# An attention and feed-forward kernel on one core: statistics in single items, later blocks normalised on ScalarE, the last output-weight chunk fetched sooner, the last projections moved to even tiles

## The chip, the core and the metric

The kernel runs on one core of a Trainium2 chip. The metric is device time in microseconds (us). Times are the median of several executions; one further execution was profiled, and everything called a row, a view or the trace comes from that one. TensorE does the matrix products (PE in the profile, its weight loads PEld), VectorE is DVE, ScalarE is ACT, GpSimd is POOL, and SyncE (SP) issues all DMAs, one after the other in program order.

## The reference, cut to what matters

A pre-norm transformer layer on 2048 tokens of width 576, all in float32: attention with 32 heads of width 18 that share one key and one value head, then a bilinear feed-forward network (FFN) with 4608 hidden features.

```python
h  = x + attention(layernorm(x)) @ wo          # 32 heads x 18 = 576 columns
n  = layernorm(h)                              # mean, variance, (h - mean) / sqrt(var + 1e-5)
h2 = h + ((n @ w_gate) * (n @ w_up)) @ w_down  # 576 -> 4608 -> 576
```

## The kernel before

**Precision and blocks.** Each float32 operand of a product is split in a rounded part and a remainder (`split`, L86: a cast on ScalarE or GpSimd, then a subtraction on VectorE), and a product is the sum of three. The 2048 tokens are cut in four blocks of 512, numbered 0 to 3. In a block, four heads make a group, so there are eight groups; a "pair" (`pair`, L456) is one key tile for two heads: two score products and one exponential on ScalarE over 128x1024 (L477).

**The FFN loop.** `ffn(b)` (L794) runs 36 tiles f = 0 to 35 of 128 hidden features. A tile has 27 steps j, each a gate and an up product (L814) on the two halves of the array; then ScalarE copies the gate sum out of PSUM (L840, the "g copy", one per tile) and VectorE multiplies it with the up sum (L844, "hf"). Two tiles make one pair for the product with w_down. After an odd tile VectorE prepares that pair (`left`, L705: four sums of halves, then a split); after the next even tile `down` (L720) runs 42 products in 14 groups, each added to the residual by VectorE (L777) or by ScalarE and GpSimd (L781, L782). So even tiles end with `down`, and odd tiles end with `left`.

**Attention of later blocks between.** While `ffn(b)` runs, the pairs of block b+1 (and, at the end, the first ones of b+2) are issued between its steps, up to eight or nine a tile (`on`, L801). They run out in `ffn(2)` near tile 24; from there on a tile has only its own work, its two sums lie in another PSUM tile ("gu"), and `down` comes ahead of the g copy instead of behind hf.

**The list of small work.** What a finished head group needs is put on a list, `self.aux`, with the round from which it is due and, for some, a condition. `run_aux` (L499) is called at step 12 of each tile ("within") and at the end of each tile but the last of a block; a call counts one round and runs at most one due item. Items with a condition run at tile ends alone. The items, for block b:

- `normalise(b, g)` (L509): divides a group's output by its sums, transposes it on VectorE and lets SP send it to its rows of `ob`; for groups 1, 3, 5 and 7 it also fetches the next chunk of wo (`load_wo`, L564) and puts `chunk` on the list.
- `chunk(b, c)` (L543): splits chunk c of 128 rows, on ScalarE and VectorE. Chunk 4, the last 64 rows, also fetches its own part of wo (L548).
- `split_wo` (L569), at the end of each `run_aux`: splits a fetched chunk of wo on GpSimd and VectorE, from two rounds after its fetch, into the only buffer for it.
- `project(b, c)` (L593): multiplies chunk c with wo into eight PSUM tiles of 128x288 (24 products, 16 for chunk 4; L608); VectorE adds each to the residual h of block b (L609). Three PSUM buffers take turns, so the fourth tile waits for the first addition.
- `all_statistics(b)` (L629), after the last chunk: per token tile two `bn_stats` and one `bn_aggr` (L103, L104), four token tiles, then 1/sqrt(var) in 13 tiny instructions (`rstd`, L106).

**From block to block.** In tile 35, at step 6, `normal(b+1)` (L634) makes the normalised tokens: four VectorE instructions of 128x576 (L640), each followed by a copy of its last 64 columns on GpSimd (L641). After tile 35, `spread(b+1)` (L644) transposes them on TensorE (L657; the tile with those copied columns comes first), and `down` of the last pair (L732) runs among these transposes. In block 0 the w_down weights are prepared once for all blocks, by GpSimd and VectorE in steps between the products of a pair's two tiles (`right_sums` and `right`, L894 and L907), and SP writes them back to DRAM.

**What sets the order.** The program is written out in this order by hand; each engine runs its own instructions in program order and waits at semaphores.

Of the kernel before, what the change touches and what calls it, by code (L numbers as in the profile page):

```python
# [58 lines left out]
class Block:  # L59
# [439 lines left out]
    def run_aux(self, limit=1, within=False):  # L499


        self.round += 1
        due = [x for x in self.aux if x[0] < self.round and (x[2] is None or not within and x[2]())][:limit]
        for x in due:
            self.aux.remove(x)
            x[1]()
        self.split_wo()

    def normalise(self, b, g, os_):  # L509
        if g == 0:  # L510
            self.ob = self.op.tile([P, 5, TB], F32, tag="ob", name=f"ob{b}")
        c = ({1: 0, 3: 1, 5: 2, 6: 3, 7: 4} if b == 0 else {1: 0, 3: 1, 5: 2, 7: 3}).get(g)
        if b and c is not None:
            self.load_wo(c)
        self.normal_heads(b, g, os_)
        del self.os[g]
        if c is not None:
            self.aux.append((self.round + (LANDING if b == 0 and c < 4 else 0), lambda: self.chunk(b, c), None))

# [23 lines left out]
    def chunk(self, b, c):  # L543

        if b == c == 0:
            self.oT = self.otp.tile([P, 8, TB], F32R, tag="oT", name=f"oT{b}")
        self.chunk_of(b, c)
        if b and c == 4:  # L548
            self.load_wo(c)
        self.aux.append((self.round, lambda: self.project(b, c),  # L550
                         lambda: b in self.h and (c in self.wos if b else self.n_pair >= self.wo_from)))

# [16 lines left out]
    def split_wo(self):  # L569

        if self.wo_r and not self.wos and self.wo_round + 1 < self.round:
            c = min(self.wo_r)
            w = self.wos[c] = self.wp.tile([P, 2, D], F32R, tag="wos", bufs=1, name=f"wos{self.round}_{c}")
            self.split(w[:, 0], w[:, 1], self.wo_r.pop(c), self.nc.gpsimd.tensor_copy)

    def load_wo_0(self):
# [16 lines left out]
    def project(self, b, c):  # L593
# [23 lines left out]
        if c == 4:  # L617
            if b == 0:
                self.normed[b] = self.mv, self.rstd(self.mv[:, :, 1], f"b{b}")
            else:  # L620
                self.aux.append((self.round, lambda: self.all_statistics(b), None))

# [5 lines left out]

    def all_statistics(self, b):  # L629
        for s in range(NQ):  # L630
            self.statistics(b, s)
        self.normed[b] = self.mv, self.rstd(self.mv[:, :, 1], f"b{b}")

    def normal(self, b):  # L634
# [3 lines left out]
        for s in range(NQ):  # L638
            xh = self.p_tile([P, 640], f"xh2_{b}_{s}") if b else self.wp.tile([P, 640], F32, tag="wdo", bufs=WD_BUFS, name=f"xh2_0_{s}")
            self.dve.tensor_scalar(xh[:, 0:D], h[:, s, :], mv[:, s, 0:1], rs[:, s:s + 1], ALU.subtract, ALU.mult)  # L640
            self.nc.gpsimd.tensor_copy(xh[:, D:], xh[:, 512:D])  # L641
            self.xh.append(xh)
# [151 lines left out]
    def ffn(self, b):  # L794
        pe, act, dve = self.pe, self.act, self.dve
        X, hid, todo = self.X, [], None
        for f in range(NF):
# [11 lines left out]
            for c in range(9):  # L809
                for wk, xk in ((0, 0), (0, 1), (1, 0)):  # L810
# [8 lines left out]
                    if j == 5 and k:  # L819
                        self.left_first(n_ - 1, hid[0])  # L820
                    if j == 12:
                        self.run_aux(within=True)
                    if b == 0 and self.first:
# [7 lines left out]
                    if j == 21 and b == f == 0:  # L831
                        self.flush(len(self.pend))
                    if j == 6 and last:
                        self.normal(b + 1)
                    j += 1
# [94 lines left out]
    def begin(self, first):  # L930
# [5 lines left out]
        self.n_pair, self.half, self.pend, self.aux, self.round = 0, [], [], [], 0  # L936
        self.p_next, self.wo_from, self.due = -1, 10 ** 6, 0.0

# [219 lines left out]
```

## Time and profile before

| | us |
|---|---|
| median of 3 executions (2342.1 to 2344.63) | 2344.12 |
| the profiled execution | 2342.39 |
| its span, from the first to the last instruction | 2340.6 |
| ScalarE busy in it | 1433.3 |
| VectorE busy in it | 1210.6 |
| GpSimd busy in it | 684.0 |

The difference of 1.8 us between the profiled execution's time and its span lies outside the first and the last instruction. In a row of a group, "xN | a, b | c" is the number of instructions, their busy us, the mean ns of one, and the us for which the engine stood idle just before them. In a row of the timeline the first two numbers are start and duration in us, and "[a <-X]" is the idle time before it and what ended it.

### The profile page before, as it was taken

The page shows a single profiled execution, that of the slowest core. Times are in us where ns is not written, and L with a number is a line of the kernel's source. Part 1 is how long each engine was busy: PE and PEld are TensorE (multiplying, and loading weights), DVE is VectorE, ACT ScalarE, POOL GpSimd, SP SyncE. Part 2 cuts the span into 40 slices and gives each one's busy share as a digit, 9 for nine tenths or more (in the row PEclk, how much of TensorE's full clock was granted, in tenths as well). Part 3 has the DMA queues.
Part 4 walks back from the last instruction along what each step waited for, and adds up shares of the span by engine and source line. Part 5 has one row for each costly group of instructions (what it writes and reads, how often), then busy time and mean ns, then how long its engine had stood idle before and what let it go on. Part 6 is the DMA issues. An engine that isn't in the chain of part 4 may idle for free.

```text
span 2340.6 us, 46187 instructions
## 1 busy us (share of the span) xinstructions
PE 2283.8 (98%) x18225; PEld 1602.6 (68%) x18225; DVE 1210.6 (52%) x2175; ACT 1433.3 (61%) x1868; POOL 684.0 (29%) x873
## 2 busy tenths in 40 slices
PE   5999999999999999999999999999999989999998
PEld 4344445666677667667777777776777678888887
DVE  7333345565656566444444445444444466556655
ACT  4888886667676765567676766667776623223332
POOL 3100001444455453222222222212222233333332
PEclk9999999999999999999999999999999999999999
DMA  4222222344444442633433443533333345655553
GB/s 140 72 65 81 75 90 81 128 147 143 148 143 143 141 146 93 197 119 123 128 123 117 123 135 107 180 109 121 113 126 122 109 145 188 203 183 171 168 180 116
DMA packets 127225, 306.59 MB, mean 131 GB/s; under 512 B 15679, under 2 KB 16447, under 8 KB 126999
## 3 DMA queue, kind: packets, MB, share of 16 engines
q1 hardware_dynamic: 126999, 303.54, 40.1%
q8 instruction: 146, 2.39, 0.4%
q14 instruction: 80, 0.66, 0.1%
HBM read 234.00 MB, written 55.67 MB: 124 GB/s over the span
## 4 chain that ended last, share of the span: by engine, by line


## 5 line engine op out<-in xcount | busy, mean ns | idle before, releaser
L477 ACT ACTIVATE P<-s 128x1024 f32<-128x1024 f32 x1024 | 1026.7, 1027 | 302.5 <-PE s L476 221.9
L814 PE MATMUL pg<-X,ws 64*128 64x512 f32 x2592 | 707.1, 391 | 0.0
L814 PE MATMUL pu<-X,ws 64*128 64x512 f32 x2592 | 707.0, 391 | 0.0
L814 PEld LDWEIGHTS pg<-X,ws 64*128 64x128 f32 x2592 | 481.4, 186 | 58.9 <-issue 1.2
L814 PEld LDWEIGHTS pu<-X,ws 64*128 64x128 f32 x2592 | 478.5, 186 | 36.7 <-DMA X<-X 0.4
L481 PE MATMUL acc<-P,V 128*32 128x512 f32 x4096 | 488.7, 598 | 0.9 <-ACT P L477 0.6
L476 PE MATMUL s<-q,kT 56*128 56x512 f32 x2048 | 436.8, 422 | 2.5 <-ACT P L477 1.8
L774 PEld LDWEIGHTS y<-wdo,room 128*128 128x128 f32 x2856 | 386.2, 188 | 48.4 <-issue 44.2
L774 PE MATMUL y<-wdo,room 128*128 128x288 f32 x2856 | 403.5, 300 | 1.1 <-DVE h L777 1.1
L781 ACT COPY tmp<-y 128x288 f32<-128x288 f32 x408 | 162.7, 400 | 342.0 <-PE y L774 326.9
L476 PEld LDWEIGHTS s<-q,kT 56*128 56x128 f32 x2048 | 194.0, 184 | 198.7 <-ACT P L477 114.4
L814 PE MATMUL gu<-X,ws 64*128 64x512 f32 x2592 | 303.1, 390 | 0.0
L782 POOL TENSOR_TENSOR x<-x,tmp 128x288 f32<-128x288 f32 x204 | 159.2, 810 | 445.5 <-ACT tmp L781 444.7
L481 PEld LDWEIGHTS acc<-P,V 128*32 128x32 f32 x4096 | 114.8, 109 | 249.2 <-issue 241.2
L814 PEld LDWEIGHTS gu<-X,ws 64*128 64x128 f32 x2592 | 248.9, 185 | 48.0 <-issue 5.2
L88 POOL CAST ws<-wr 128x1152 fp32r<-128x1152 f32 x144 | 171.6, 1191 | 329.7 <-PE pg L814 111.4
L782 POOL TENSOR_TENSOR h<-h,tmp 128x288 f32<-128x288 f32 x204 | 159.4, 812 | 371.0 <-ACT tmp L781 370.7
L89 DVE TENSOR_TENSOR ws<-wr,ws 128x1152 fp32r<-128x1152 f32 x144 | 204.4, 1419 | 82.4 <-POOL ws L88 82.4
L844 DVE TENSOR_TENSOR hf<-pu,g 128x512 f32<-128x512 f32 x96 | 66.3, 690 | 264.5 <-ACT g L840 261.2
L777 DVE TENSOR_TENSOR x<-x,y 128x288 f32<-128x288 f32 x272 | 117.4, 453 | 146.4 <-PE y L774 146.4
L777 DVE TENSOR_TENSOR h<-h,y 128x288 f32<-128x288 f32 x272 | 118.2, 454 | 114.9 <-PE y L774 112.2
L89 DVE TENSOR_TENSOR room<-S,room 128x1024 fp32r<-128x1024 f32 x68 | 86.0, 1265 | 149.2 <-ACT room L88 149.2
(169 smaller groups left out, 1734.6 us busy)
## 6 DMA issues: line engine op xcount, KB each, us to landing
wdo<-wd_dram SPq DMA_DIRECT2D x369, 288.0 KB
wr<-in_wgu_dram SPq DMA_DIRECT2D x144, 576.0 KB
wd_dram<-wdo SPq DMA_DIRECT2D x123, 288.0 KB
q<-q_dram SPq DMA_DIRECT2D x64, 216.0 KB
raw<-in_wd_dram SPq DMA_DIRECT2D x36, 288.0 KB
q_dram<-qs SPq DMA_DIRECT2D x16, 504.0 KB
X<-X SPq DMA_DIRECT2D x28, 256.0 KB
x<-in_x_dram SPq DMA_DIRECT2D x16, 288.0 KB
```

The source lines that it names most:

```text
L88: (copy or self.cast)(hi, src)
L89: self.dve.tensor_tensor(lo, src, f32(hi), ALU.subtract)
L476: self.pe.matmul(s_[:, i], self.kT[o:o + 56, t * P:(t + 1) * P], q[o:o + 56, pr], start=True, stop=True)
L477: self.act.activation(p_, s_, AF.Exp, scale=SCALE)
L481: self.pe.matmul(acc[32 * j:32 * j + 32, :], self.V[:, t, :], Ps[j // 2][:, j % 2, :], start=(t == 0), stop=(t == NT - 1), skip_group_chec ...
L774: pe.matmul(y[:, :HD], m[:, t * P:(t + 1) * P], k, start=(first and j == 0), stop=(j == 2), skip_group_check=True)
L777: dve.tensor_tensor(hs, hs, y[:, :HD], ALU.add)
L781: act.copy(z, y[:, :HD])
L782: pool.tensor_tensor(hs, hs, z, ALU.add)
L814: pe.matmul(ps, w[o:o + 64, wk, c], X[o:o + 64, xk, c], start=(j == 0), stop=(j == 26))
L844: dve.tensor_tensor(hf, pu, g, ALU.mult)
```

## The change

It has five parts, all in how the FFN blocks are served.

1. **Statistics in single items.** `all_statistics` becomes four items, one a token tile. For blocks 1 and 2 they can run within a tile or at its end. For block 3 they run only within odd tiles, two in one call, and the 13 instructions of `rstd` are an item of their own (`scales`). `scales` also makes -mean/sqrt(var), one more tiny instruction.
2. **Normalising on ScalarE.** For blocks 1 to 3, `normal` uses four ScalarE activations (Identity, with scale 1/sqrt(var) and bias -mean/sqrt(var)) in place of the four VectorE instructions. Block 0 stays on VectorE.
3. **wo sooner.** The fetch of wo's chunk 4 is issued right after the split of chunk 3, not by chunk 4's own item.
4. **Even ends.** The projections of block 3 run only at the ends of even tiles (`self.odd` holds whether the last finished tile was odd). Chunk 0 of later blocks is due two rounds later than before.
5. **Tile 35.** No item runs within the last tile of blocks 0 to 2. In block 0 all steps of `right` for the last pair are issued at step 6, ahead of `normal(1)`, and no longer between later steps.

In the order of the program this moves the items so ("end 8" is the end of tile 8, "in 8" its step 12; all other items stay where they were):

| item | before | after |
|---|---|---|
| block 1, in ffn(0): chunk 0, project 0 | end 6, end 7 | end 7, end 8 |
| wo chunk 4 fetched, project 4 | in 32, end 33 | in 31, end 32 |
| statistics of block 1 | all at end 34 | in 33, end 33, in 34, end 34 |
| block 2, group 0 normalised | in 34 of ffn(0) | in 0 of ffn(1) |
| block 2, in ffn(1): chunk 0, project 0 | end 3, end 4 | end 4, end 5 |
| wo chunk 4 fetched, project 4 | in 29, end 30 | in 28, end 29 |
| statistics of block 2 | all at end 31 | in 30, end 30, in 31, end 31 |
| block 3, group 0 normalised | in 31 of ffn(1) | in 32 of ffn(1) |
| block 3, group 1 normalised | in 35 of ffn(1) | in 0 of ffn(2) |
| block 3, in ffn(2): chunk 0 | in 0 | end 1 |
| projects 0 to 4 | ends 1, 9, 17, 25, 27 | ends 2, 10, 18, 26, 28 |
| wo chunk 4 fetched | in 26 | in 25 |
| statistics of block 3 | all in 28 | two in 29, two in 31, `scales` in 33 |

```diff
@@ run_aux
-        due = [x for x in self.aux if x[0] < self.round and (x[2] is None or not within and x[2]())][:limit]
+        due = [x for x in self.aux if x[0] < self.round and (x[2] is None or within == (x[2] == self.within) and x[2]())][:limit]
...
+    def within(self):
+        return not self.odd
@@ normalise
-            self.aux.append((self.round + (LANDING if b == 0 and c < 4 else 0), lambda: self.chunk(b, c), None))
+            self.aux.append((self.round + (LANDING if b == 0 and c < 4 else 2 if b and c == 0 else 0), lambda: self.chunk(b, c), None))
@@ chunk
-        if b and c == 4:
-            self.load_wo(c)
         self.aux.append((self.round, lambda: self.project(b, c),
-                         lambda: b in self.h and (c in self.wos if b else self.n_pair >= self.wo_from)))
+                         lambda: b in self.h and (c in self.wos and not (self.odd and b == NB - 1) if b else self.n_pair >= self.wo_from)))
@@ split_wo
             self.split(w[:, 0], w[:, 1], self.wo_r.pop(c), self.nc.gpsimd.tensor_copy)
+            if c == 3:
+                self.load_wo(4)
@@ project
-                self.aux.append((self.round, lambda: self.all_statistics(b), None))
+                last = b == NB - 1
+                for i in range(4):
+                    self.aux.append((self.round + i // 2, lambda i=i: self.some_statistics(b, i), self.within if last else None))
+                if last:
+                    self.aux.append((self.round + 2, lambda: self.scales(b), self.within))
...
+    def some_statistics(self, b, s):
+        self.statistics(b, s)
+        if s == NQ - 1 and b < NB - 1:
+            self.scales(b)
+
+    def scales(self, b):
+        mv, r = self.mv, self.rstd(self.mv[:, :, 1], f"b{b}")
+        self.dve.scalar_tensor_tensor(mv[:, :, 0], mv[:, :, 0], -1.0, r, ALU.mult, ALU.mult)
+        self.normed[b] = mv, r
@@ normal
-            self.dve.tensor_scalar(xh[:, 0:D], h[:, s, :], mv[:, s, 0:1], rs[:, s:s + 1], ALU.subtract, ALU.mult)
+            if b:
+                self.act.activation(xh[:, 0:D], h[:, s, :], AF.Identity, bias=mv[:, s, 0:1], scale=rs[:, s:s + 1])
+            else:
+                self.dve.tensor_scalar(xh[:, 0:D], h[:, s, :], mv[:, s, 0:1], rs[:, s:s + 1], ALU.subtract, ALU.mult)
@@ ffn
-                    if j == 12:
-                        self.run_aux(within=True)
+                    if j == 12 and not last:
+                        self.run_aux(2 if b == NB - 2 and k else 1, within=True)
...
                     if j == 6 and last:
+                        if b == 0 and self.first:
+                            drain(parts)
                         self.normal(b + 1)
...
+            self.odd = k
             if f < NF - 1:
                 self.run_aux()
```

More of the change, by code (lines that the diff above doesn't have):

```diff
@@ L627, in statistics @@
         self.ln_stats(self.h[b][:, s, :], self.mv[:, s, :], s, f"b{b}")
[L629 to L632, printed above, removed]
+    def some_statistics(self, b, s):
[6 more added lines that the diff above has]
+        self.normed[b] = mv, r
     def normal(self, b):
@@ L936, in begin @@
         self.n_pair, self.half, self.pend, self.aux, self.round = 0, [], [], [], 0
-        self.p_next, self.wo_from, self.due = -1, 10 ** 6, 0.0
+        self.p_next, self.wo_from, self.due, self.odd = -1, 10 ** 6, 0.0, 0
     def blocks(self):
```

## The prediction, made before the changed kernel ran

> **What bounds the kernel now.** I read the page first.
>
> ```profile
> PE 2283.8 (98%) x18225; PEld 1602.6 (68%) x18225; DVE 1210.6 (52%) x2175; ACT 1433.3 (61%) x1868; POOL 684.0 (29%) x873
> ```
>
> TensorE is busy 98% of the span: a change that leaves its products alone can only win the time in which it waits or runs slowly. So next come its waits, longest in total first (us in total, times, longest); these belong to what the diff touches:
>
> ```profile
> PE yo L608 <- DVE x L609: 6.7, 6, 1.8
> PE yo L608 <- DVE h L609: 5.7, 2, 3.0
> ...
> PE tx L657 <- POOL xh L641: 3.4, 3, 3.1
> ```
>
> Projections wait for VectorE's additions (12.4 us; block 3's two waits are 5.7 of it), and the transposes at a block's end once wait 3.1 us for normalised tokens. A wait is not the whole loss, so I measure whole stages: the view by windows, each cut from the start of one g copy (L840) to the start of another; this one begins the third.
>
> ```profile
> 1384.15 0.58 ACT L840 COPY g<-pg 128x512 f32<-128x512 f32 x1
> ```
>
> The columns are bounds, length, busy us and count of PE, PEld, DVE, ACT and POOL, then the granted clock.
>
> ```profile
> 1354.37:1372.10 17.73, 17.73 (x148) 13.23 (x147) 7.92 (x16) 11.28 (x17) 5.94 (x8) 1.00 0.55 170
> 1372.10:1384.15 12.05, 12.05 (x106) 7.64 (x110) 6.68 (x10) 10.31 (x13) 1.59 (x2) 1.00 0.41 108
> 1384.15:1405.45 21.30, 21.15 (x172) 16.87 (x168) 9.84 (x20) 11.57 (x18) 5.92 (x8) 1.00 0.45 139
> 1417.49:1438.50 21.01, 20.71 (x164) 16.69 (x160) 10.93 (x24) 11.28 (x17) 5.96 (x8) 1.00 0.42 132
> 1648.78:1664.26 15.48, 15.48 (x130) 11.08 (x134) 8.60 (x16) 9.80 (x13) 0.98 (x1) 1.00 0.12 40
> 501.26:517.84 16.58, 15.70 (x130) 10.95 (x134) 11.62 (x20) 9.92 (x13) 4.65 (x6) 1.00 0.48 163
> 905.98:922.85 16.87, 15.05 (x122) 10.34 (x126) 12.79 (x25) 9.92 (x13) 2.25 (x3) 1.00 0.54 196
> 1930.80:1949.13 18.33, 18.33 (x153) 17.05 (x152) 11.11 (x19) 5.56 (x13) 6.95 (x9) 1.00 0.54 181
> 1878.94:1903.77 24.83, 22.20 (x177) 18.92 (x176) 17.29 (x30) 6.69 (x15) 8.02 (x10) 1.00 0.53 172
> 1903.77:1930.80 27.03, 23.11 (x168) 20.09 (x167) 20.78 (x53) 5.54 (x12) 7.52 (x10) 0.94 0.42 122
> 1495.96:1514.64 18.68, 18.47 (x143) 15.43 (x146) 9.39 (x13) 12.48 (x17) 5.13 (x7) 1.00 0.76 208
> 938.57:962.76 24.19, 20.30 (x143) 16.95 (x146) 13.41 (x22) 12.19 (x17) 8.02 (x14) 0.93 0.76 224
> ```
>
> In order: a tile whose window holds a `down` takes 17.73, one without 12.05 (call these even and odd end). The third has an even-end projection: 21.30 - 17.73 = **3.57**. The fourth is a last chunk (16 products) at an even end: 21.01 - 17.73 = **3.28**. The fifth, an odd end in ffn(2): 15.48 - 12.05 = **3.43**. The sixth and seventh are odd ends in ffn(0), where VectorE also prepares w_down: chunk 0 costs 16.58 - 12.05 = **4.53**, chunk 4 16.87 - 12.05 = **4.82**. The eighth is a pair of tiles with no attention left, 18.33; the same with block 3's chunk 3 at an odd end costs **6.50** more, with chunk 4 and then all statistics **8.70** more. Last come two passages from block to block with equal PE counts (x143): 1 to 2 takes 18.68, 0 to 1 takes 24.19, **5.51** more. What sets the dear stages apart from their cheap likes, 0.96 + 1.54 + 2.93 + 5.42 + 5.51 = 16.4 us, is about what the edits can reach.
>
> In two windows the clock is below 1.00; the first row below lies in the earlier printed of them, behind its wait, the second holds block 3's other wait:
>
> ```profile
> 1915.00:1917.00 2.00, 2.00 (x11) 1.66 (x10) 1.79 (x5) 0.00 (x0) 0.00 (x0) 0.58 0.00 0
> 1887.00:1891.00 4.00, 1.37 (x10) 1.28 (x10) 3.91 (x11) 1.66 (x2) 0.00 (x0) 1.00 0.18 73
> ```
>
> After the two waits of 3 us TensorE ran at half clock, which cost 0.07 x 24.19 = 1.7 us and 0.06 x 27.03 = 1.6 us; after block 3's shorter wait (5.7 - 3.0 = 2.7 us) it did not. The waits that I forecast below, 1.3 us at most, are shorter still, so I count these 3.3 us as won with the waits.
>
> The Trainium skill's "TensorE: Matmul & The Clock Gate", section "Part 1: The HAM clock gate (the "warmup" mystery)", has the clock halved after an idle window of about 3.4 us, for about as long. By that figure neither wait here would have halved it, and the sum below would be 3.3 us smaller; the rows say that waits of 3.0 and 3.1 us did, and the rows decide.
>
> **The change part by part.** All against the profiled execution (2342.39 us; span 2340.6).
>
> *Projections that move.* Block 1's chunk 0 goes from an odd to an even end: 4.53 to 3.57, -1.0 (bounds 0 and -1.1, if it costs 4.53 as now or 3.43). Its chunk 4: 4.82 to 3.28, -1.5 (bounds -0.3 and -2.5: 4.53, or 16/24 of 3.43, which is 2.3). Block 2's chunk 0 goes the other way, 3.57 to 3.43: -0.1 (up to +1.0, at 4.53). Its chunk 4 at an odd end has a row only in ffn(0), 4.82; the other bound is 2.3. Eight additions are more than 16 products, so I take 3.0, nearer to 24 products' 3.43: -0.3 (-1.0 to +1.5). Block 3's chunks 0 to 2 lose, 3.43 to 3.57: +0.4 together (0 to +0.8). Sum **-2.5**.
>
> *Block 3's last two.* Why they cost so much stands on VectorE:
>
> ```profile
> 1886.42 0.69 DVE L844 TENSOR_TENSOR hf<-gu,g 128x512 f32<-128x512 f32 x1 [1.81 <-ACT g L840]
> ...
> 1889.22 3.26 DVE L609 TENSOR_TENSOR h<-h,yo 128x288 f32<-128x288 f32 x8
> ...
> 1938.30 0.69 DVE L844 TENSOR_TENSOR hf<-gu,g 128x512 f32<-128x512 f32 x1 [3.37 <-ACT g L840]
> ```
>
> At an odd end the additions stand behind hf and `left`, 2.8 us (1889.22 - 1886.42); at an even end only hf (0.69) is ahead. Eight additions take 3.26, about what 24 products take, so no second wait forms. I take the even costs: chunk 3 6.50 to 3.6 (**-2.9**, bounds -2.0 and -3.1, at 4.53 and 3.43), chunk 4 8.70 to 3.3 (**-5.4**, bounds -3.9 and -6.4, at 4.82 and 2.3).
>
> The statistics leave chunk 4's `down`, whose additions they held up. Their new places, odd tiles 29, 31 and 33, have an idle VectorE between step 5 and hf: 3.37 us, the third row. Costs, from the passage 0 to 1:
>
> ```profile
> 932.60 0.81 DVE L103 BATCH_NORM_STATS2 bsb<-x 128x6 f32<-128x288 f32 x2
> ...
> 936.47 0.17 DVE L113 TENSOR_SCALAR vb<-mvb 128x4 f32<-128x4 f32 x1
> ...
> 938.66 0.16 DVE L125 SCALAR_TENSOR_TENSOR yb<-tb,yb 128x4 f32<-128x4 f32 x1
> 938.74 1.36 DVE L89 TENSOR_TENSOR ws<-wr,ws 128x1152 fp32r<-128x1152 f32 x1
> 940.01 0.68 DVE L89 TENSOR_TENSOR room<-hf,room 128x512 fp32r<-128x512 f32 x1
> 940.61 2.04 DVE L640 TENSOR_SCALAR xh<-x,mvb,yb 128x576 f32<-128x576 f32 x4
> 943.42 2.21 DVE L921 TENSOR_TENSOR wdo<-raw,wdo 128x288 fp32r<-128x288 f32 x4 [0.77 <-POOL wdo L918]
> ```
>
> Four token tiles take 936.47 - 932.60 = 3.87, so two take 1.9; `rstd` takes 938.82 - 936.47 = 2.35, with the added instruction (0.16) 2.5. Both fit into 3.37: cost 0. Without that cover they would push hf by at most their own 1.9 or 2.5.
>
> *Passage 0 to 1.* Today VectorE starts four statistics at 932.60 and gets to `normal` at 940.61; GpSimd copies follow, and TensorE, free at 938.75, waits:
>
> ```profile
> 941.82 0.33 PE L657 MATMUL tx<-C,xh 128*128 128x128 f32 x1 [3.07 <-POOL xh L641]
> ```
>
> ```profile
> 941.32 1.70 POOL L641 COPY xh<-xh 128x64 f32<-128x64 f32 x4 [7.25 <-DVE xh L640]
> 942.96 1.99 POOL L918 CAST wdo<-raw 128x288 fp32r<-128x288 f32 x4
> ```
>
> ```profile
> 13.67 3.15 ACT L181 ACTIVATE xh<-x,n,ya 128x576 f32<-128x576 f32 x4 [3.47 <-DVE n L173]
> ```
>
> Afterwards one statistic is left (932.60 to 933.6), then `rstd` and the new instruction, to 936.3. The activation is in the trace at the start (L181, same shape): four in 3.15, so 936.4 to 939.5. The GpSimd copies (0.43 each) follow, the last done at 940.0; `right`'s casts, now ahead of them (1.99), come right behind `down`'s last addition and the ws cast (1.19 in a row below), and are over when ScalarE's first is. TensorE's fourth transpose starts at 940.0 instead of 943.0 (941.32 + 1.70): 3 us won, and the half clock (1.7) with it. Late next is hf: ScalarE's g copy moves from 938.57 to 939.5 (over at 940.1), and VectorE has from 936.3 on its two splits (1.36 and 0.68) and `right`'s four subtractions (2.21, now ahead of hf), to 940.6. Before, hf came after 943.42 + 2.21 = 945.6, so it too is earlier; against the calm passage I put 0.3 for it. 3.0 + 1.7 - 0.3 = **-4.4** (bounds 0, and -5.5, the whole difference to the other passage).
>
> *Passages 1 to 2 and 2 to 3.* TensorE doesn't wait for xh there, ScalarE has no exponentials in tile 35, and its 3.15 us fit ahead of the transposes: 0. In 1 to 2 group 1's VectorE work goes from in front of hf: **-0.2** (0 to -0.2: TensorE is idle for 18.68 - 18.47 there).
>
> *wo sooner.* SP now has to wait at that fetch until VectorE has split chunk 3, as `wor` has one buffer; behind it in SP's queue stand weight fetches. Cost 0, by rows given with the third rival.
>
> Sum: -2.5 - 2.9 - 5.4 - 4.4 - 0.2 = **-15.4**, so 2327.0 for a profiled execution. That one ran 1.73 below the median of the runs; against the median, 2344.12, it is **2328.7**. With every term at its lesser end (0, 0.3, -1.0, -1.5, -0.8, 2.0, 3.9, 0, 0) 2.9 us are won, with every one at its greater end (1.1, 2.5, 0.1, 1.0, 0, 3.1, 6.4, 5.5, 0.2) 19.9.
>
> **Rivals.**
>
> *ScalarE is late (2335.5).* It needs 3.15 for what VectorE did in 2.04. If the four start only 2 us later than I work out (statistics held by casts ahead), TensorE still waits 3 us and the clock falls: the 4.4 and 0.2 are gone, and 1.1 each (3.15 - 2.04) are lost in the other two passages. 15.4 - 4.6 - 2.2 = 8.6 won, 2335.5. For it: the chain from 932.60 has no slack. Against it: ScalarE has no exponentials there, and only one split of hf in its queue ahead.
>
> The Trainium skill's "ScalarE: Activation LUTs", section "Rules for kernel authors", speaks for this rival: additions and products belong on VectorE, not ScalarE. The rows agree on the speed; they also show VectorE as the late one here.
>
> *The late projections still wait (2335).* `down`'s last additions, hf and eight additions meet at the even end, and PSUM buffers come free no sooner: chunks 3 and 4 win only what the statistics and the half clock took, about 2. 15.4 - 8.3 + 2 = 9.1 won, 2335.0. Against it: the even rows (3.57, 3.28) hold the same meeting.
>
> *SP holds up the weights (2349 or more; slower).* The fetch of wo chunk 4 waits for VectorE and keeps ws's source (`wr`) behind it. The rows of SP's waits, and of GpSimd's casts of wr:
>
> ```profile
> SPq L678 <- DVE ws L89: 724.9, 95, 19.9
> ```
>
> ```profile
> L88 POOL CAST ws<-wr 128x1152 fp32r<-128x1152 f32 x144 | 171.6, 1191 | 329.7 <-PE pg L814 111.4 <-PE gu L814 91.9 <-PE pu L814 88.9
> ```
>
> SP already waits up to 19.9 us, and the casts were released by TensorE (292 of 329.7 us), not by a DMA. `wr` has two buffers, so a fetch has about a tile, 12.05, in hand; beyond that each us of delay costs TensorE one, three times. To be slower by 0.2% it needs (15.4 + 4.7) / 3 = 6.7 us beyond the slack each time.
>
> *It doesn't do what it says (2342).* The instruction order shows the moves, so only a full give-back is left: each wait reappears at the next tile.
>
> **How the numbers follow.** Forecast 0.71 (2328.7), ScalarE late 0.11, late projections 0.07, no effect 0.07 (where the two before land together), SP 0.04. The range goes from all terms at their greater ends, 2344.1 - 19.9 = 2324.2, to the two smaller gains, 2335.5 and 1 us for the spread of the runs: 2336.5. What lies above it, no effect and SP, holds 0.11. 0.2% is 4.7 us, about what a measurement of this kernel can tell from no change: faster 0.88, same 0.08, slower 0.04.
>
> **What would show it.** In the changed profile: no wait of TensorE over 1.5 us behind the start; granted clock 1.00 between the start and the end; passage 0 to 1 near 19.8 us; block 3's chunks 3 and 4 near 3.6 and 3.3 us above 18.3; VectorE's statistics in odd tiles with idle time left before hf. A wait of tx for xh of 2 us or more, yo waits for h as long as now, or casts of wr released by a DMA would make it wrong.

## The result, and the profile after

| | before | after |
|---|---|---|
| median, us | 2343.89 (2342.10 to 2344.63, 4 runs) | 2327.43 (2327.23 to 2327.73, 4 runs) |
| the profiled execution, us | 2342.39 | 2327.44 |
| its span, us | 2340.6 | 2325.6 |

One more execution of the kernel before was measured beside the changed one, hence four. The ratio is 0.9931, with a 95% interval of [0.9914, 0.9948]. The forecast was 2328.7 us, faster, in a range of 2324.2 to 2336.5. The line numbers have moved: the g copy is now L860, the projection L612 and L613, the transposes L675, the last pair's products L750.

The first line of the page of the changed kernel shows each engine's busy time, its share of the span and its instructions:

```profile
PE 2280.0 (98%) x18225; PEld 1600.4 (69%) x18225; DVE 1199.9 (52%) x2166; ACT 1443.0 (62%) x1880; POOL 688.3 (30%) x873
```

TensorE has the same 18225 products and is busy 3.8 us less (2283.8 before); the other 11.2 us of the 15.0 were idle time. Its waits in the changed kernel (us in total, times, longest):

```profile
PE yo L612 <- DVE x L613: 4.1, 4, 1.5
...
PE tx L675 <- POOL xh L659: 1.2, 3, 0.5
...
PE yo L612 <- DVE h L795: 0.7, 4, 0.3
```

Block 3's waits for additions into h (5.7 us, twice) are down to small ones of 0.3 us at most, and the 3.1 us for xh have become three short ones. Of the 4.1 us left for x, 1.5 lie in the start phase, as before, and 2.6, in three waits, are block 1's, whose chunks 1 to 3 still stand at odd ends. The view by windows of the changed kernel (columns as in the prediction) has the stages that the prediction priced:

```profile
514.56:535.86 21.30, 21.16 (x172) 16.50 (x170) 13.08 (x26) 11.28 (x17) 10.11 (x16) 1.00 0.25 90
888.62:909.46 20.84, 20.55 (x164) 16.32 (x160) 13.21 (x29) 11.33 (x18) 10.21 (x16) 1.00 0.26 92
1879.49:1901.59 22.10, 21.95 (x178) 19.55 (x176) 16.50 (x29) 6.18 (x13) 7.61 (x10) 1.00 0.55 191
1901.59:1923.40 21.81, 21.36 (x170) 18.68 (x168) 15.76 (x33) 5.56 (x11) 6.89 (x9) 1.00 0.47 154
939.12:956.84 17.72, 17.27 (x140) 15.18 (x143) 9.23 (x16) 12.19 (x17) 4.89 (x7) 1.00 0.98 308
1489.56:1507.34 17.78, 17.74 (x143) 15.30 (x146) 8.85 (x14) 12.20 (x16) 4.56 (x6) 1.00 0.77 210
```

The first two are block 1's chunks 0 and 4 at even ends: 21.30 - 17.73 = 3.57 and 20.84 - 17.73 = 3.11 above a tile that has a `down` alone. The next two are block 3's chunks 3 and 4 over two tiles: 3.77 and 3.48 above 18.33, where they were 6.50 and 8.70. The fifth is the passage 0 to 1, here at full clock (24.19 before); since the g copy at its head now stands behind ScalarE's normalising, the tile ahead of it (0.34) has grown from 15.72 to 17.61, so the two are always taken together below: 39.91 before, 35.33 here. The sixth is the passage 1 to 2 (18.68 before).

Rival three has its answer in the page and in the waits. GpSimd's casts of wr in the changed kernel, then what ended the idle time before them (first line the group's row, second from the view of that tile):

```profile
L88 POOL CAST ws<-wr 128x1152 fp32r<-128x1152 f32 x144 | 171.3, 1190 | 326.9 <-PE pu L832 119.2
```

```profile
  DMA wr<-in_wgu_dram: 21.5, 4
```

DMAs ended 21.5 us of the idle time in that view in four places, in the kernel before 21.6 in three. The view counts all engines, and the fourth place is 0.8 us of TensorE's weight loads; GpSimd's own casts of wr waited 20.6 us in three places. The earlier fetch of wo did not hold up the weights. One cast of a wo chunk, at 1517 us, waits 8.9 us for its DMA, which none did before, but TensorE has no wait over 0.2 us between 1500 and 1545.

### The profile page after: what moved, and what is told of

It is laid out like the page before. It is cut to its first block, busy times and chain, and to the rows that moved or that the text cites. A ratio compares the mean times of both kernels' runs of the same rounds, so it can differ in the third digit from the quotient of the medians.

```text
span 2325.6 us, 46197 instructions
## 1 busy us (share of the span) xinstructions
PE 2280.0 (98%) x18225; PEld 1600.4 (69%) x18225; DVE 1199.9 (52%) x2166; ACT 1443.0 (62%) x1880; POOL 688.3 (30%) x873
## 4 chain that ended last, share of the span: by engine, by line
PE 93%; DVE 3%; ACT 1%; issue 1%; POOL 1%; DMA 0%; SPq 0%; ACTq 0%; DVEq 0%; POOLq 0%
PE acc L481 19%; PE y L792 17%; PE pg L832 15%; PE gu L832 13%; PE s L476 12%; PE pu L832 10%; PE psq L331 3%; PE yo L612 3%; PE y L750 1%; ACT P L477 1%; DVE wdo L942 1%; PE ye L750 0%; PE tx L675 0%; DVE bsa L103 0%; PE psg L361 0%
```

## The experiments

Each kernel is told by its edit against the changed kernel or the kernel before. Intervals run from one g copy to the next; "tile 0.35" is the stretch from the g copy of tile 35 of ffn(0) to the next one.

**1. Normalising on VectorE again** (part 2 undone; against the changed kernel)

```diff
-                self.act.activation(xh[:, 0:D], h[:, s, :], AF.Identity, bias=mv[:, s, 0:1], scale=rs[:, s:s + 1])
+                self.dve.tensor_scalar(xh[:, 0:D], h[:, s, :], rs[:, s:s + 1], mv[:, s, 0:1], ALU.mult, ALU.add)
```

> The changed kernel with its normalisation of blocks 1 to 3 back on VectorE (part 2 undone alone). Theory (the gain at the passage 0 to 1 needs ScalarE, because VectorE's queue there still holds two splits and right's four subtractions ahead of the normalisation): TensorE's wait for the normalised tokens there comes back, about 4 us instead of under 1.3, its clock falls to half for 3.4 us, and the time is 4.5 us above the changed kernel, near 2332. Rival (the single statistics alone freed the passage, ScalarE is only another place): within 1 us of the changed kernel, 2327.4 to 2328.4, clock 1.00 there.

Measured: 2332.17 us (2330.33 to 2332.36), 4.7 above the changed kernel. In the trace tiles 0.34 and 0.35 are 3.9 longer than in the changed kernel's first profile, 2.4 longer than in its second (experiment 9), and 0.7 and 1.7 come from the start phase, whose program is the same: over all profiles the first g copy begins between 400.1 and 402.6. The passage in this kernel, as a window, and two of VectorE's rows, the first ahead of it:

```profile
937.89:961.34 23.45, 19.48 (x143) 16.73 (x146) 13.48 (x24) 12.28 (x16) 6.21 (x10) 0.93 0.80 240
```

```profile
933.00 1.93 DVE L113 TENSOR_SCALAR vb<-mvb 128x4 f32<-128x4 f32 x1
...
940.58 2.04 DVE L656 TENSOR_SCALAR xh<-x,yb,mvb 128x576 f32<-128x576 f32 x4
```

The four instructions start at 940.58, almost where they did in the kernel before (940.61), and 0.7 us later than there when counted from the g copy of tile 34, although the statistics are early: the two splits and `right`'s subtractions, now ahead of them, fill VectorE, and `rstd`'s first instruction alone takes 1.93 us beside GpSimd's casts (experiment 2 has more on that). TensorE waits 3.7 us and the half clock is back: the theory holds. Early statistics win only 0.7 us of the passage (39.91 to 39.18) as long as VectorE also normalises.

**2. The statistics of blocks 1 and 2 in one call** (part 1 undone for these)

```diff
-                for i in range(4):
-                    self.aux.append((self.round + i // 2, lambda i=i: self.some_statistics(b, i), self.within if last else None))
+                if not last:
+                    self.aux.append((self.round + 3, lambda: [self.some_statistics(b, i) for i in range(4)], None))
+                for i in range(4 if last else 0):
+                    self.aux.append((self.round + i // 2, lambda i=i: self.some_statistics(b, i), self.within))
```

> The changed kernel with the four statistics of blocks 1 and 2 in one call again, at the place of the last one (part 1 undone for these blocks, ScalarE still normalises). Theory: VectorE starts the 13 small instructions 2.9 us later, ScalarE too; TensorE waits about 4 us in the passage 0 to 1 and runs at half clock behind it: 2.9 + 1.7, less what slack there is, 4 to 4.6 us above the changed kernel, near 2332; nothing in the passage 1 to 2. Rival (ScalarE alone freed the passage): at most 1 us above the changed kernel.

Measured: 2329.37 us (2328.56 to 2329.50), +1.9; in the trace tiles 0.34 and 0.35 together +2.8, against the changed kernel's second profile (9), in which the clock fell as here, +1.4. That is between the two expectations. The rows of VectorE and GpSimd say why. The changed kernel, VectorE and then GpSimd:

```profile
931.25 0.81 DVE L103 BATCH_NORM_STATS2 bsb<-x 128x6 f32<-128x288 f32 x2
...
932.34 0.44 DVE L113 TENSOR_SCALAR vb<-mvb 128x4 f32<-128x4 f32 x1
...
933.43 0.46 DVE L116 TENSOR_SCALAR vb<-vb 128x4 f32<-128x4 f32 x1
...
934.29 0.16 DVE L120 TENSOR_TENSOR tb<-tb,vb 128x4 f32<-128x4 f32 x1
...
935.87 0.17 DVE L646 SCALAR_TENSOR_TENSOR mvb<-mvb,yb 128x4 f32<-128x4 f32 x1
```

```profile
932.69 1.55 POOL L939 CAST wdo<-raw 128x288 fp32r<-128x288 f32 x4
```

This kernel:

```profile
934.48 0.17 DVE L113 TENSOR_SCALAR vb<-mvb 128x4 f32<-128x4 f32 x1
...
936.86 0.16 DVE L648 SCALAR_TENSOR_TENSOR mvb<-mvb,yb 128x4 f32<-128x4 f32 x1
```

In the changed kernel `rstd` begins while GpSimd does `right`'s casts, and its first instructions take 0.34 to 0.46 us each in place of 0.17; when the casts end at 934.24 they fall to 0.16. From L113's start to the end of the last one it takes 3.70 us, against 2.54 here, where the four statistics stand beside the casts. So single items take three statistics out of the way (2.8 us, by the four's 3.87 in the prediction) and lose 1.2 of it to GpSimd.

**3. `right`'s steps between the later steps again** (part 5 undone in this one point)

```diff
-                        if b == 0 and self.first:
-                            drain(parts)
                         self.normal(b + 1)
```

> The changed kernel with right's last steps back between the later products of tile 35 of block 0, behind the normalisation (part 5 undone in this point). Theory: GpSimd's copies wait for ScalarE until 940, right's casts and VectorE's subtractions come after them, so hf is 2 to 3 us later and the last down's first products wait for it: 1.5 to 2.5 us above the changed kernel, near 2329.4. Rival (the order of right is of no matter, since TensorE has 2.2 us of transposes ahead): 0 to 0.5 us above.

Measured: 2330.11 us (2328.71 to 2330.65), +2.7; tiles 0.34 and 0.35 together +2.9 against the first profile of the changed kernel and +1.5 against the second (9), in which the clock fell as here. TensorE's transposes hardly wait; the wait stands behind them. VectorE and GpSimd, then TensorE, in this kernel:

```profile
938.59 2.21 DVE L940 TENSOR_TENSOR wdo<-raw,wdo 128x288 fp32r<-128x288 f32 x4 [1.97 <-POOL wdo L937]
940.72 0.68 DVE L862 TENSOR_TENSOR hf<-pu,g 128x512 f32<-128x512 f32 x1
```

```profile
942.10 0.53 PE L750 MATMUL y<-wdo,room 128*128 128x288 f32 x2 [1.08 <-ACT room L88]
```

GpSimd casts for `right` only behind its four xh copies, VectorE waits 1.97 us for that with hf behind it, and the last pair's products wait for the rounded hf. The theory holds, with the median a little above its range.

**4. Normalising on ScalarE alone** (against the kernel before)

```diff
+        mv, r = self.mv, self.rstd(self.mv[:, :, 1], f"b{b}")
+        self.dve.scalar_tensor_tensor(mv[:, :, 0], mv[:, :, 0], -1.0, r, ALU.mult, ALU.mult)
...
+            if b:
+                self.act.activation(xh[:, 0:D], h[:, s, :], AF.Identity, bias=mv[:, s, 0:1], scale=rs[:, s:s + 1])
...
```

> The kernel before with part 2 alone: blocks 1 to 3 normalised on ScalarE, statistics in one call, all else as before. Theory: in the passage 0 to 1 the four activations start at 938.9, when the statistics are done, and end at 942.1; the last copy lands 0.4 us sooner than before, TensorE still waits over 3 us and its clock still falls: 0.3 to 1.2 us faster than the kernel before, with up to 0.7 of it in the passage 1 to 2. Rival (ScalarE frees the passage by itself): 4 to 5 us faster than before, near 2339.

Measured: 2342.95 us (2341.49 to 2346.90, 10 runs) beside 2343.64 for the kernel before, ratio 0.9999 [0.9989, 1.0008]. In the trace tiles 0.34 and 0.35 take 39.33 in place of 39.91: the clock still falls, as expected, but behind waits of 2.8 us in four, the longest 1.7, and not behind one of over 3. What is lost when part 2 is undone (4.7) isn't there when it is done alone: the four statistics and `right` stand in the same passage, and its whole gain needs all three parts. The passage 1 to 2, where none of them matters, has the whole gain of the change (18.68 to 17.77).

**5. The even ends alone** (against the kernel before)

```diff
-                         lambda: b in self.h and (c in self.wos if b else self.n_pair >= self.wo_from)))
+                         lambda: b in self.h and (c in self.wos and not (self.odd and b == NB - 1) if b else self.n_pair >= self.wo_from)))
...
+            self.odd = k
...
```

> The kernel before with the even-end rule for block 3 alone (projections at ends 2, 10, 18, 26, 28; the statistics of block 3 still all in one call, now within odd tile 29). Theory: chunks 3 and 4 cost 3.6 and 3.3 us in place of 6.5 and 8.7, chunks 0 to 2 lose 0.5 together, and the statistics cost nothing within an odd tile even in one call: 7.8 us faster than before, near 2336. Rival (the statistics need to be in single items): hf of tile 29 is 3 us late and TensorE waits for it, so 4 to 5 us faster only, near 2339.

Measured: 2337.43 us (2335.85 to 2338.77, 9 runs) beside 2344.20, ratio 0.9972 [0.9963, 0.9982]; -6.2 us in the trace. Between the two: chunks 3 and 4 come to even ends as in the changed kernel, but all four statistics now stand in tile 29, and tile 2.29 takes 13.21 in place of 11.45.

**6. Block 3 free to use odd ends** (part 4 undone, but for the two rounds of chunk 0; against the changed kernel)

```diff
-                         lambda: b in self.h and (c in self.wos and not (self.odd and b == NB - 1) if b else self.n_pair >= self.wo_from)))
+                         lambda: b in self.h and (c in self.wos if b else self.n_pair >= self.wo_from)))
```

> The changed kernel with block 3's projections free to run at odd ends again (chunk 0 stays at end 2, chunks 1, 2, 3 go to 9, 17, 25, chunk 4 to the even end 26; statistics in 27, 29, scales in 31). Theory: chunk 3 alone pays, 6.5 for 3.6, chunks 1 and 2 win 0.2 each: 2.5 us above the changed kernel, near 2329.9; TensorE waits 2.6 us for h once. Rival (the late projections were dear because of the statistics near them, not of the odd end): within 0.5 us of the changed kernel.

Measured: 2331.11 us (2329.96 to 2331.70), +3.7. Chunk 3 at the odd end 25, as a window of this kernel and of the kernel before:

```profile
1879.63:1899.11 19.48, 16.86 (x119) 14.95 (x119) 12.77 (x24) 5.16 (x11) 5.24 (x7) 0.91 0.39 126
```

```profile
1885.80:1903.77 17.97, 15.34 (x119) 13.58 (x120) 11.67 (x23) 5.18 (x11) 4.53 (x6) 1.00 0.40 130
```

The same 119 products behind the same wait of 2.6 to 2.7 us: with the half clock 1.5 us more than without. The odd end itself costs what it cost before. So the theory's 2.5 us are there, and the rest is the half clock behind them.

**7. Block 3's statistics in one call** (part 1 undone for block 3)

```diff
-                for i in range(4):
+                for i in range(0 if last else 4):
...
-                    self.aux.append((self.round + 2, lambda: self.scales(b), self.within))
+                    self.aux.append((self.round, lambda: [self.some_statistics(b, i) for i in range(4)] + [self.scales(b)], self.within))
```

> The changed kernel with the four statistics and the scales of block 3 in one call within odd tile 29. Theory: VectorE has 3.9 + 2.5 = 6.4 us of them where 3.4 are idle, so hf and left of tile 29 end 3 us later, but nothing on TensorE needs them before the down of tile 30, some 6 us on: 0, within 0.4 us of the changed kernel. Rival (single items matter for block 3, as the last words of the prediction's part on them had it): up to 3 us above the changed kernel.

Measured: 2329.49 us (2328.84 to 2329.63), +2.1; tile 2.29 takes 13.42 in place of 11.43. My theory fell and the rival holds. VectorE's hf in the changed kernel, then VectorE, GpSimd and TensorE in this one:

```profile
1924.03 0.69 DVE L864 TENSOR_TENSOR hf<-gu,g 128x512 f32<-128x512 f32 x1 [3.05 <-ACT g L860]
```

```profile
1923.51 1.07 DVE L119 TENSOR_TENSOR tb<-yib 128x4 f32<-128x4 f32 x1
...
1926.27 0.68 DVE L864 TENSOR_TENSOR hf<-gu,g 128x512 f32<-128x512 f32 x1
```

```profile
1923.41 1.15 POOL L88 CAST ws<-wr 128x1152 fp32r<-128x1152 f32 x1 [7.97 <-PE gu L832]
```

```profile
1930.94 0.40 PE L792 MATMUL y<-wdo,room 128*128 128x288 f32 x1 [0.23 <-DVE room L89]
1932.58 3.62 PE L792 MATMUL y<-wdo,room 128*128 128x288 f32 x25 [1.24 <-DVE h L795]
```

With two statistics in the tile VectorE still stands idle for 3.05 us before hf. The other two and `scales` need 1.9 + 2.5 = 4.4 by the prediction's prices, and one instruction of `rstd` takes 1.07 us in place of 0.16, until GpSimd's cast is over; hf comes 2.2 us later, and VectorE, busy from hf up to `down`'s additions, hands this on: TensorE waits for h.

**8. Better ends** (against the changed kernel: block 1's chunks 0 to 2 at even ends only, block 3's chunks 0 to 2 free)

```diff
-                         lambda: b in self.h and (c in self.wos and not (self.odd and b == NB - 1) if b else self.n_pair >= self.wo_from)))
+                         lambda: b in self.h and (c in self.wos and not (self.odd and (b == 1 and c < 3 or b == NB - 1 and c > 2)) if b else self.n_pair >= self.wo_from)))
```

> The changed kernel with the even-end rule put by stage: block 1's chunks 1 and 2 at even ends too (16 and 24 instead of 15 and 23), block 3's chunks 1 and 2 at odd ends (9 and 17), chunks 3 and 4 at even ends as changed. Theory (an odd end costs 4.5 us while VectorE prepares w_down, 3.4 afterwards while attention runs, an even end 3.6 throughout): 2 x 0.9 + 2 x 0.2 = 2.2 us below the changed kernel, near 2325.2. Rival (at an even end of block 0 GpSimd's and VectorE's load from w_down makes a second projection there as dear): within 0.5 us of it.

Measured: 2326.81 us (2324.18 to 2327.15, 5 runs), ratio to the kernel before 0.9927 [0.9914, 0.9941]. In the trace the chunks win 0.8 each in block 1 (-4.48 + 3.66 and -4.48 + 3.61) and 0.2 each in block 3, 2.1 together, as expected. The median shows 0.6 of it (1.1 against the executions of experiment 9), and the ranges overlap: in this profile the clock fell in the passage, which took 1.5 us more than in the changed kernel's first.

**9. The changed kernel once more**

> The changed kernel as it is, for more executions and a second profile. Theory (the half clock behind the last wait of the passage 0 to 1 comes in most executions, not in all): in three of four profiles with the same passage the interval was 19.2 us with granted clock 0.91, in the changed kernel's own 17.72 with 1.00. So here 19.2 is likelier than 17.7, chance 3 in 4; the median stays at 2327 to 2328. Rival (the changed kernel's passage is 17.7 by nature and the other kernels' edits lengthen it): 17.7 again, clock 1.00.

Measured: 2327.90 us (2327.14 to 2328.29, 5 runs), ratio 0.9935 [0.9921, 0.9948]. The passage took 19.16, at a clock of 0.91. TensorE in it, in slices of 1 us (length, PE busy, PEld, DVE, ACT and POOL, clock), first in the changed kernel's first profile, then in this one:

```profile
937.00:938.00 1.00, 0.71 (x4) 0.14 (x1) 1.00 (x3) 1.00 (x2) 0.65 (x2) 1.00 0.00 0
938.00:939.00 1.00, 0.45 (x2) 0.26 (x2) 1.00 (x3) 1.00 (x2) 0.35 (x2) 1.00 0.65 138
939.00:940.00 1.00, 0.55 (x4) 0.36 (x5) 0.79 (x3) 0.69 (x2) 0.33 (x1) 1.00 0.99 376
940.00:941.00 1.00, 1.00 (x11) 1.00 (x10) 0.41 (x1) 0.56 (x2) 0.00 (x0) 1.00 0.99 385
```

```profile
937.00:938.00 1.00, 0.33 (x1) 0.14 (x1) 1.00 (x4) 1.00 (x2) 0.50 (x2) 1.00 0.54 101
938.00:939.00 1.00, 0.53 (x3) 0.34 (x4) 0.79 (x3) 0.83 (x2) 0.32 (x1) 1.00 0.97 355
939.00:940.00 1.00, 1.00 (x9) 1.00 (x8) 0.55 (x1) 0.42 (x1) 0.00 (x0) 0.82 0.95 373
940.00:941.00 1.00, 1.00 (x7) 1.00 (x6) 0.77 (x2) 1.00 (x3) 0.00 (x0) 0.50 1.05 403
```

The same program with the same three short waits (1.2 us): once the clock stays, once it falls to half for about 3 us, which costs 1.4 us. Of five profiles with these instructions in the passage (this kernel twice, 6, 7 and 8) it fell in four. Its profiled time is only 0.85 us longer than the first's (2328.29 and 2327.44), since the first had the slower start phase (first g copy at 401.82, here 400.82).

**10. Normalising on both engines** (against the changed kernel: block 1's last token tile on VectorE, right behind `scales`)

```diff
+        if b == 1:
+            self.xh_3 = self.p_tile([P, 640], f"xh2_{b}_3")
+            self.dve.tensor_scalar(self.xh_3[:, 0:D], self.h[b][:, 3, :], r[:, 3:4], mv[:, 3, 0:1], ALU.mult, ALU.add)
...
+        if b == 1:
+            self.nc.gpsimd.tensor_copy(self.xh_3[:, D:], self.xh_3[:, 512:D])
-        for s in range(NQ):
+        for s in range(NQ - (b == 1)):
...
```

> The changed kernel with block 1's last token tile normalised on VectorE, right behind the scales, and the other three on ScalarE. Theory: TensorE's gaps before the second, third and fourth transpose (0.31, 0.45 and 0.45 us) fall to two or fewer, 0.4 to 0.8 us won, and with so little idle time the clock stays at 1.00 in the profile (interval 17.0 to 17.4); with the half clock (1.5 us) gone from about three executions in four, about -1.9 on the median: 2325.5. Rival A (the clock falls behind this shorter wait as well): -0.8 alone, 2326.6, clock about 0.91 in the interval. Rival B (VectorE's 0.5 us more ahead of its splits, right and hf becomes the last wait): 0 to -0.3 from the wait, 2327.2 or above.

Measured: 2327.74 us (2326.97 to 2328.90, 5 runs), no gain; the theory fell, and so did rival A's gain, though the clock fell as rival A had it. The time lies where rival B put it, but the last wait is not the one for hf. VectorE, GpSimd and TensorE's wait in this kernel:

```profile
935.69 1.35 DVE L89 TENSOR_TENSOR ws<-wr,ws 128x1152 fp32r<-128x1152 f32 x1
```

```profile
935.84 1.30 POOL L657 COPY xh<-xh 128x64 f32<-128x64 f32 x1 [2.47 <-DVE xh L650]
```

```profile
PE tx L682 <- POOL xh L664: 1.3, 1, 1.3
```

GpSimd's copy of 64 columns took 1.30 us in place of some 0.4: it ran from 935.84 to 937.14, until 0.1 us after VectorE's subtraction of 1152 columns ended. The other copies came behind it, and TensorE waits 1.3 us ahead of its first transpose in place of 1.2 ahead of the next three. The wait only changed its place, and the clock fell behind it: tiles 0.34 and 0.35 take 36.67 (36.74 in experiment 9).

**11. 8 and 10 together**

> The kernel before this one with block 1's chunks 0 to 2 projected at even ends only and block 3's chunks 0 to 2 free to take odd ends (better_ends). Theory: the two gains are in different tiles and add up: -2.1 and -1.9 from 2327.4, about 2323.5. Rival (a gain in one place returns as a wait in the other, or the half clock falls as often): not below 2325.

Measured: 2324.80 us (2323.68 to 2327.17, 5 runs), ratio 0.9924 [0.9911, 0.9938], between the two expectations. In this profile the clock stayed (passage 18.77, after a tile 0.34 of 16.83), behind the same wait of 1.3 us as in 10, and the four chunks win what they won in 8. By experiment 10 its edit brings nothing, so what goes beyond 8's -2.1 is put down to the clock, which the medians alone can't show.

**12. Token by token** (against 8: the passage's 20 transposes of block 1 in the order of the token tiles)

```diff
+        steps = [(c, k, n, t, s) for c, n, t in tx for k in range(n) for s in range(NQ)]
+        if b == 1:
+            steps.sort(key=lambda x: x[4])
...
```

> better_ends (2326.8 us) with the 20 transposes of the passage 0 to 1 taken token tile by token tile, so that TensorE has five for each tile that ScalarE delivers. Theory (what is late next is the last pair's rounded hf: in the changed kernel's trace ScalarE casts it until 941.06 and VectorE subtracts until 941.79, and the transposes end just then, at 941.73): the waits for xh shrink from 1.2 us to 0.3 or less, but TensorE then waits about 0.7 to 1.2 us ahead of the last pair's products, so 0 to -0.5 us: 2326.3 to 2326.8, the interval 0.34 plus 0.35 not below 36.3 with the half clock or 34.8 without. Rival (the transposes alone bound the passage): -1.2 us, and as nothing is idle there the half clock (1.5 us) goes as well: 2324.5 or less, the clock 1.00 in the interval.

Measured: 2325.12 us (2324.33 to 2325.70, 5 runs), ratio 0.9920 [0.9906, 0.9933]. TensorE in this kernel:

```profile
935.89 2.96 PE L676 MATMUL tx<-C,xh 128*128 128x128 f32 x20
938.61 0.63 PE L752 MATMUL y<-wdo,room 128*128 128x288 f32 x3
939.54 0.53 PE L752 MATMUL y<-wdo,room 128*128 128x288 f32 x2 [0.30 <-ACT room L88]
940.27 0.40 PE L752 MATMUL y<-wdo,room 128*128 128x288 f32 x1 [0.20 <-DVE room L89]
940.87 3.34 PE L752 MATMUL y<-wdo,room 128*128 128x288 f32 x23 [0.20 <-DVE X L684]
```

The 20 transposes run without a wait, and the products behind them wait for the rounded hf, as the theory said. Tiles 0.34 and 0.35 take 35.33 us (17.58 + 17.75), exactly what they take in the changed kernel's first profile, also at full clock (17.61 + 17.72). So the chain to the rounded hf bounds the passage, and the waits for xh cost nothing of their own. The median lies 1.2 us below the theory's range all the same. What the median has won over 8, 1.7 us, fits a clock that no longer falls; the idle time is now spread in waits of 0.3 us at most. One profile doesn't show how often it falls, and the ranges of 8 and 12 overlap.

## Why the prediction was right, point by point

In the table, "forecast" is the prediction's term and "measured" the change of the intervals concerned, from the profile before to the profile after, in us.

| step | forecast | measured |
|---|---|---|
| block 1, chunks 0 and 4 to even ends | -1.0, -1.5 | -0.9, -1.6 |
| block 2, chunks 0 and 4 to odd ends | -0.1, -0.3 | -0.2, -0.3 |
| block 3, chunks 0 to 2 to even ends | +0.4 | +0.8 |
| block 3, chunk 3 | -2.9 | -2.7 |
| block 3, chunk 4 and the statistics | -5.4 | -5.2 |
| passage 0 to 1 | -4.4 | -4.6 (second profile -3.2) |
| passage 1 to 2 | -0.2 | -0.9 |
| sum | -15.4 | -15.5; all tiles -16.2 |

- **The price list by position held.** A projection costs 3.57 at an even and 3.43 at an odd end, 4.5 and more where VectorE also prepares w_down: read off before, found again after to 0.3 us each or better. Experiments 6 and 8 moved chunks both ways at these prices, so this step is shown.
- **The statistics at no cost in odd tiles** held because they were split over three tiles. Experiment 7 shows the limit: behind two statistics VectorE has 3.05 us left before hf, and the other two with `scales` don't fit.
- **The passage 0 to 1: the order held, one time in it did not.** ScalarE and TensorE in the changed kernel, the second row from the fourth transpose on:

```profile
936.07 3.15 ACT L656 ACTIVATE xh<-x,mvb,yb 128x576 f32<-128x576 f32 x4 [4.70 <-DVE mvb L646]
```

```profile
939.66 2.08 PE L675 MATMUL tx<-C,xh 128*128 128x128 f32 x17 [0.45 <-POOL xh L659]
```

These times look like the forecast's (936.4 and 940.0), but that is luck. The forecast used the timeline of the kernel before, and in the profile after this stretch begins 1.3 us sooner (g copy of tile 34 at 921.51 in place of 922.85). Counted from that g copy, the fourth transpose starts after 18.2 us; 17.2 was forecast, and before it was 20.2. So 2.0 of the 3.0 us came. The missing 1.0 is `rstd` with its new instruction, put at 2.5 us: it took 3.70 beside GpSimd's casts. Behind the fourth transpose 2.6 us were won where 1.7 - 0.3 = 1.4 was forecast: the clock stayed full, and waits of 0.3 and 0.2 us for X and the rounded hf are gone. In the second profile, with the half clock, 1.1 were won there.
- **Which part wins the passage.** Experiments 1, 2 and 3 take the three parts out one at a time, and the median loses 4.7, 1.9 and 2.7 us. At like clocks (0.91 to 0.93 in the passage) tiles 0.34 and 0.35 take 39.91 before, 39.33 with ScalarE alone (4), 39.18, 38.11 and 38.20 with one part missing, and 36.74 in the changed kernel's second profile: each part counts, and the 3.2 us belong to the three together. What was late next was named, hf, and 12 shows that its chain already bounds the passage: without the waits for xh it takes no less. No run takes out the earlier fetch of wo, chunk 0's two rounds, or the rule that no item runs within tile 35 by itself; what they bring is read from the tiles' intervals only.
- **The half clock: this step failed.** "The waits that I forecast below, 1.3 us at most, are shorter still, so I count these 3.3 us as won with the waits." The 1.6 us at block 3's chunk 4 were won, since no long wait is left there. The 1.7 us of the passage are won only at times: behind 1.2 us of waits the clock fell in four profiles of five. Of the signs named at the prediction's end, full clock held in one of the changed kernel's two profiles; no wait behind the start phase is over 0.9 us. That the sum fitted is partly luck: the profile after had full clock in the passage, worth 1.4 us, and a start phase 1.2 us longer (first g copy at 401.82, before 400.61), in which the program is the same.
- **Passage 1 to 2: mis-sized.** I bounded the gain by TensorE's idle time there, 18.68 - 18.47 = 0.2 us; it was 0.9. The busy time itself fell, from 18.47 to 17.74 with 143 products in both windows, so idle time in a window was no upper bound; which products were stretched is not shown. Experiments 1 and 4 both have 17.8 there, so either taking the four instructions or taking the head group's work away from VectorE suffices.
- **Why the median fell by 16.5, the profiled time by 15.0.** In 45 executions of the kernel before, measured beside the experiments, the mean granted clock is 0.992 to 0.995; the 17 at 0.995 have a median of 2341.89, the 18 at 0.993 one of 2344.45. The profiled one is of the upper group, the medians are not. In the nine executions of the changed kernel it is 0.995 to 0.997. This fits a change that took away waits behind which the clock could fall, of which the median saw more than the one profile. No execution at 0.993 was profiled, so where its clock fell is not shown.
- **The rivals.** ScalarE was 1.0 us later than forecast (counted as above), not the 2 that the first rival needs; the eight additions at the even end cause waits of 0.3 us at most; SP waited longer for ws (773.2 us in place of 724.9), while GpSimd's casts of wr waited for DMAs no longer than before (20.6 and 21.6 us). Nothing was given back: the priced stages make up 15.5 of the 16.2 us that all tiles won.

## What to carry to other kernels

Price a piece of small work by the place where it runs, by comparing stages with and without it, and move it to the cheaper place; here that list forecast each moved projection to 0.3 us or better. Where three engines hand on to each other behind a block's last product, a part done alone may win nothing: write the chain with its times for all engines, and look at which chain ends just behind the one that is shortened. A bound taken from idle time inside a window can be too small, as busy time may fall too; compare whole windows with the same products. And before you trust a time that came out as forecast, count it from the same event in both profiles.

## What the runs showed of the hardware

- **The clock falls by chance behind short waits.** Behind waits of 1.2 us in a stretch of 3 us TensorE was granted half clock in four profiles of five, behind one wait of 2.6 to 2.7 us in two of three (1.5 us each time), behind 3.0 to 3.7 us each of the five times that it was seen behind the start phase. Behind one wait of 1.3 us it fell in experiment 10 and stayed in 11, and it stayed behind the 1.8 us ahead of block 1's chunk 4 in the kernel before. The Trainium skill's "TensorE: Matmul & The Clock Gate", section "Part 1: The HAM clock gate (the "warmup" mystery)", says that the window of about 3.4 us runs freely, so that the same program meets it at different places; the toss between executions of one program agrees with that. That a whole window has to be idle does not agree: here about two fifths of 3 us were (1.2 us). No run here shows where such a window begins.
- **GpSimd and VectorE hold each other up.** A copy of 64 columns took 1.30 us beside a subtraction of 1152 columns and ended 0.1 us behind it; `rstd`'s instructions took 0.34 to 0.46 us beside GpSimd's casts and 0.16 or 0.17 after them, one in experiment 1 took 1.93, and one in experiment 7 took 1.07 and ended 0.02 us behind GpSimd's cast. The Trainium skill's "SBUF — State Buffer", section "Who interferes with whom", has the two share a port pair under an exclusive lock, where a VectorE instruction with two inputs in SBUF stands against a GpSimd instruction that reads SBUF; the ends of the copy and of experiment 7's instruction agree. Moving `right`'s casts ahead thus had a price of 1.2 us in the changed kernel that the prediction didn't have.
